# Attention: a unit's sums copied by two engines, half the columns each; root steps and turns moved in the projections

## The chip, the cores and the metric

The kernel runs on one core of a Trainium2 chip. The metric is the device time of one execution in microseconds, the median of several runs. The engines are TensorE (PE in the profile; its weight loads are PEld), VectorE (DVE), ScalarE (ACT), GpSimd (POOL) and SyncE (SP), which issues nearly all DMAs. Each engine works through its own queue in order; semaphores tie the queues together. TensorE writes its results into eight banks of PSUM, 512 float32 columns for each of 128 partitions.

## The reference

A transformer block on 2048 tokens of 640 numbers: layer norm, attention with 32 heads of 20 numbers, residual, layer norm, gated feed-forward of width 1728, residual.

```python
qkv = (x @ wqkv).reshape(B, S, 3, H, Dh).transpose(2, 0, 3, 1, 4)      # x: layer norm of the input
scores = jnp.einsum("bhqd,bhkd->bhqk", q, k) * (Dh ** -0.5)
p = softmax(scores, axis=-1)
o = jnp.einsum("bhqk,bhkd->bhqd", p, v)
h = x + o.transpose(0, 2, 1, 3).reshape(B, S, D) @ wo
h2 = h + (silu(n @ w_gate) * (n @ w_up)) @ w_down                      # n: layer norm of h
```

## The kernel before

**Three stages.** The projections (to about 325 us) make queries, keys and values; the attention (to about 1460 us) runs over 32 units; the rest is the output projection and the feed-forward part. Float32 is split into a high and a low part (`split`, L96: ScalarE copies the high part, another engine subtracts to get the low one, the "second part"), and products are the sum of three.

**The attention.** A unit `u` is a group of four heads and a chunk of 512 queries; it runs over 16 key tiles `kt`. A step of this loop has, for each head, one score product (`scores`, L1379, to a bank out of four) and its exponential on ScalarE (L1390); the weighing of the tile before it (`weigh`, L1392: probabilities times values, with a column of ones that yields the denominators), which adds up over the 16 tiles in one bank of its own (`acc`); and three maximum products for later units (`max_one`, L235, three banks in turn), each reduced by VectorE (L245). The order within a step is written out by hand in `ORDER`, three strings and their mirror images: `s` and `S` are scores, `m` and `M` maximum products, `W` the weighing, always last:

```python
ORDER = ("sMsSmSmW", "SmMsMsSW", "mSmMsSsW")
```

When the weighing of a unit's last tile is issued, in the first step of the next unit, `row_sums` (L1402) copies the bank to the tile `o` and lets SP bounce the rows of denominators (L1407); a few steps later they are inverted, spread over the heads' rows, multiplied in by GpSimd (L1429) and stored. There is one such bank, so the next unit's first weighing waits until the copy is done. VectorE's queue at this place holds the reductions of the step that ends, then, where a unit's maxima are complete, `max_all` (L249), then the reductions of the next step.

**The projections.** The tokens are taken in four chunks of 512. Work is a list of 72 slots: `first`, `none`, then `block` slots (a 128-row block of queries or keys of a chunk) and `value` slots. `begins(n)` is the slot at which chunk `n` is due: 10, 28 and 46. A planner, the class `Halves` (`pe`), keeps a modelled clock for each engine (`pe.free`, `pe.now()`) while the program is written and orders the instructions by it: products of the two halves of the array side by side, and in between, as filler, products of the maxima for which keys have landed. `second_part` (L661) chooses the engine of a second part by the modelled ends on GpSimd (1.3 us) and VectorE (0.75 us).

A chunk's tokens are normalized by items in the list `lns` (from `norm`, L759): four of statistics, six of the reciprocal root (Newton steps on VectorE, two instructions each, four numbers a row), four that apply it (VectorE for the first two chunks, GpSimd for the last two). Then come five turns (`flip`, L787): TensorE transposes a 128-column block of the chunk, ScalarE copies it twice, the second part follows. At the end of each slot the main loop issues up to two items (four in slots 4 to 6) and one turn, once all items are gone and the plan says that they are done; in the slot after `begins(n)` it issues all that are left, since the chunk's first block follows.

Of the kernel before, what the change touches and what calls it, by code (L numbers as in the profile page):

```python
# [13 lines left out]
AF = mybir.ActivationFunctionType  # L14
# [11 lines left out]
CH = 512  # L26
NC = S // CH
# [23 lines left out]
def tile_block(ctx: ExitStack, tc: tile.TileContext, x, wqkv, wo, wg, wu, wd, out):  # L51
    nc = tc.nc
# [77 lines left out]
    def stats(pool, src, mv):  # L130
        st = pool.tile([P, 2, 6], F32, name="st")
        for i in range(2):
            nc.vector.bn_stats(st[:, i, :], src[:, i * HALF : (i + 1) * HALF])  # L133
        nc.vector.bn_aggr(mv, st)


    NU = NG * NC
# [15 lines left out]
    ends = {}  # L153
# [185 lines left out]
    with tc.tile_pool(name="pa", bufs=2) as pa:  # L339
# [33 lines left out]
        def raw_place():  # L373
            return place(raw_tile().rearrange("p a b -> p (a b)")[:, : 2 * CH], nc.vector)
# [151 lines left out]
        def next_pair():  # L526
# [2 lines left out]
            queues = (others, early) if first else (early, others)  # L529
            return next((queue for queue in queues if queue and queue[0][0]()), None)  # L530

        SECOND = (("pool", 1.3), ("vector", 0.75))

        class Halves:
# [125 lines left out]

            def second_part(self, after):  # L661
                ends = [max(self.free[e], after, self.now()) + us for e, us in SECOND]
                if ends[1] + 1.0 < ends[0] and self.free["vector"] < after + 0.5:
                    return nc.vector, self.use("vector", SECOND[1][1], after)
                return nc.gpsimd, self.use("pool", SECOND[0][1], after)

# [70 lines left out]
        pe = Halves()  # L737
# [21 lines left out]
        def norm(c):  # L759

            mv = pa.tile([P, TPC, 2], F32, name="mv")
            r, steps = rstd_steps(pa, mv[:, :, 1], TPC, "a")

            def apply(t):
                (nc.gpsimd if c > 1 else nc.vector).tensor_scalar(
                    xs[c * TPC + t], xs[c * TPC + t], mv[:, t, 0:1], r[:, t : t + 1],
                    op0=ALU.subtract, op1=ALU.mult,
                )

            return (  # L770
                [
                    (("vector", 1.1), lambda t=t: stats(pa, xs[c * TPC + t], mv[:, t, :]), c)
                    for t in range(TPC)
                ]
                + [(("vector", 0.35), lambda f=f, g=g: (f(), g()), c) for f, g in zip(steps[::2], steps[1::2] + [lambda: None])]
                + [
                    (("pool", 2.55) if c > 1 else ("vector", 0.75), lambda t=t: apply(t), c)
                    for t in range(TPC)
                ]
            )  # L780
# [148 lines left out]
        def begins(c):  # L929
            return FIRST + (c - 1) * PHASE  # L930
# [9 lines left out]
        lns, flips, normed, x_at = [], [], 0.0, {1: 0.0}  # L940
        finish_at = len(work)
        for at, (kind, c, *which) in enumerate(work):
            slot[0] = at
            if at < 9:
                for i in range(split_at[at], split_at[at + 1]):
                    split_w(i + 2)
                    if i % 2 == 1 and loaded < 8:
                        load_w(loaded)
                        pe.sp(kb=655)
                        loaded += 1  # L950
            if at == 6:
                assert 9 not in raws
                own_places.insert(0, raw_place())
            if at == 9:
                assert not raws
                free_places.extend(raw_place() for _ in range(3))
            for n in range(1, NC):
                if at == (2 if n == 1 else begins(n) - 15):
                    lns = norm(n)
                if at == n == 1:  # L960
                    fill_rest()
                if n > 1 and at == begins(n) - 16:
                    assert not flips
                    load_x(n)
                    x_at[n] = pe.sp(n=4, kb=1310) + 0.3
            if kind == "first":
                first_blocks()
            elif which:
                (query_key if kind == "block" else value)(c, *which)
            for n in range(1, NC):  # L970
                if at == (7 if n == 1 else begins(n) - 3):
                    pe.finish_before(n - 1)
                    new_z(n)
                    flips = [(n, k) for k in range(ND)]
            if at == begins(NC - 1) + 15:
                pe.finish_before(NC - 1)
                z = zs[NC - 2][1]
                for i in (0, 2):
                    free_places.append(z[:, i : i + 2])
                z = pa.tile([P, ND, CH], F32R, name="z_hi")  # L980
                es += [z[:, :2], z[:, 2:4]]
                es[:] = [e for e in es if e is not stored(third)]
            if at == begins(NC - 1) + 4:
                assert not flips
                z = pa.tile([P, TPC, D], F32R, name="xt", bufs=1).rearrange("p t d -> p (t d)")
                free_places.extend(place(z[:, i * 2 * CH : (i + 1) * 2 * CH]) for i in range(2))
            if at >= LAST_QUARTER:
                for places in (free_places, own_places):
                    for i, q in enumerate(quarters):
                        if any(p is q for p in places):  # L990
                            places[:] = [p for p in places if p is not q]
                            cs = slice(i * CH, (i + 1) * CH)
                            fill_ones(k_stk[0], cs)
                            ready = pe.use("pool", 1.9, place_at.get(id(q), 0.0)) + 0.2
                            coming.append((ready, cs))
                            returned.append(i)
                back()
            for u, when in enumerate((5, begins(1) + 14, begins(2) + 14)):
                if at == when - 4:
                    es[:] = [e for e in es if all(e is not stored(q) for q in lent[:u])]  # L1000
                if at == when:
                    assert landed[0, 0, u] == GD
                    load_queries(u)
                    queries_at[u] = pe.sp(n=4, kb=750) + 4.5
            if 0 in ends:
                finish_at = min(finish_at, at + 2)
                if at == finish_at:
                    max_finish(0)
            if at == len(work) - 4:
                relus[:] = [r for r in relus if r is not third_relu]  # L1010
            if at == len(work) - 3:
                pe.finish_seconds()
                load_values(0, 0, NT - TPC)
            last = any(at == begins(n) + 1 for n in range(1, NC))
            for _ in range(99 if last else 4 if 4 <= at < 7 else 2):
                if at >= 2 and lns and (pe.now() >= x_at[lns[0][2]] or last):
                    normed = pe.use(*lns[0][0], normed) + 0.2
                    lns.pop(0)[1]()
            for _ in range(99 if last else 1):
                if flips and not lns and (pe.now() >= normed or last):  # L1020
                    flip(*flips.pop(0))
            if at == len(work) - 6:
                nc.scalar.activation(
                    pa.tile([P, 1], F32, name="exp_table"), eps_t, AF.Exp
                )
# [373 lines left out]
                tile_position=(0, 32 * j),  # L1399
            )  # L1400

    def row_sums(acc, *queues):  # L1402
        o = pc.tile([P, CH], F32, name="o", bufs=1)
        nc.scalar.activation(o, acc, AF.Copy)
        r = pc.tile([P, 16], F32, name="r")
        for j in range(G):
            queues[j % len(queues)].dma_start(  # L1407
                r[32 * j : 32 * j + 32, :],
                o[32 * j + DH : 32 * j + DH + 1, :].rearrange("r (p f) -> r p f", p=32),
            )  # L1410
        return o, r
# [24 lines left out]
    todo, tail, accs, closing, ended, now = [], [], {}, {}, [], [0]  # L1436
# [16 lines left out]
    def weigh_next():  # L1453
        u, kt, probs = todo.pop(0)
        if kt == 0:
            accs[u] = banks[:, acc_place]
        weigh(u, kt, probs, accs[u])
        if kt == NT - 1:
            queues = [nc.sync] if u + 1 < NU else [nc.scalar, nc.sync]
            tail.append((u, *row_sums(accs.pop(u), *queues)))  # L1460

    extra = []
    preparing = prepare_weights()
# [1 line left out]
    for u in range(NU):  # L1465
        g, c = divmod(u, NC)
        if g == NG - 1 and c >= 2:
            _, first, ln, flips, _ = ahead
            extra = [*first, *ln, lambda: None, *flips]
        for kt in range(NT):  # L1470
# [45 lines left out]
            if g == NG - 1 and c >= 1:  # L1516
                at = 8 if sooner else NT - 4
# [19 lines left out]
    while todo:  # L1537
        weigh_next()
    u, o, r = tail.pop()
# [466 lines left out]
    for e, (pair, f) in enumerate(ELEMENTS):  # L2006
        steps = 6 if f == NF - 1 else 8
        number, begin = RATES.get(e, (14 if e else 0, 0))
        each = spread_over(number, steps, begin)
        at = [0]  # L2010
# [90 lines left out]
```

## Time and profile before

| | us |
|---|---|
| runs (3): median, lowest, highest | 2024.7, 2023.99, 2026.38 |
| the profiled execution: its time, its span | 2026.52, 2024.7 |
| busy over the span: PE, DVE, ACT, POOL | 2002.5, 1620.2, 1460.2, 779.8 |

The span runs from the first to the last instruction of the profiled execution. Groups are read as: line, engine, operation, tile written <- tiles read, shapes, count | busy us in all, mean ns of one | idle us of the engine before them, and what ended it. In a timeline the first two numbers are the start and the length in microseconds, and "x4" means that four such instructions were put together. TensorE's clock was granted in full throughout.

### The profile page before, as it was taken

The page shows a single profiled execution, that of the slowest core. Times are in us where ns is not written, and L with a number is a line of the kernel's source. Part 1 is how long each engine was busy: PE and PEld are TensorE (multiplying, and loading weights), DVE is VectorE, ACT ScalarE, POOL GpSimd, SP SyncE. Part 2 cuts the span into 40 slices and gives each one's busy share as a digit, 9 for nine tenths or more (in the row PEclk, how much of TensorE's full clock was granted, in tenths as well). Part 3 has the DMA queues.
Part 4 walks back from the last instruction along what each step waited for, and adds up shares of the span by engine and source line. Part 5 has one row for each costly group of instructions (what it writes and reads, how often), then busy time and mean ns, then how long its engine had stood idle before and what let it go on. Part 6 is the DMA issues. An engine that isn't in the chain of part 4 may idle for free.

```text
span 2024.7 us, 39120 instructions
## 1 busy us (share of the span) xinstructions
PE 2002.5 (99%) x13714; PEld 1237.8 (61%) x13714; DVE 1620.2 (80%) x3257; ACT 1460.2 (72%) x2944; POOL 779.8 (39%) x1075
## 2 busy tenths in 40 slices
PE   8999999999999999999999999999999999999998
PEld 7898896333333333333333333345598888888888
DVE  8869678888888888888888888886378666676667
ACT  4888888999999999999999999986633222212221
POOL 4454451243524334344520011011146444764555
PEclk9999999999999999999999999999999999999999
DMA  7866663433443534435333122221159654974542
GB/s 234 257 198 192 190 191 108 135 116 117 140 128 106 161 117 142 145 123 166 123 134 102 33 71 73 81 62 49 46 185 323 206 189 154 352 272 159 204 148 93
DMA packets 205205, 304.91 MB, mean 151 GB/s; under 512 B 47648, under 2 KB 82720, under 8 KB 203984
## 3 DMA queue, kind: packets, MB, share of 16 engines
q1 hardware_dynamic: 204768, 302.24, 45.7%
q8 instruction: 109, 1.79, 0.4%
q14 instruction: 88, 0.72, 0.1%
q10 hardware_dynamic: 240, 0.17, 0.0%
HBM read 205.78 MB, written 95.68 MB: 149 GB/s over the span
## 4 chain that ended last, share of the span: by engine, by line
PE 95%; DVE 2%; ACT 1%; issue 1%; POOL 1%; DMA 0%; SPq 0%; ACTq 0%; DVEq 0%; POOLq 0%
PE banks L1394 25%; PE banks L1384 17%; PE banks L1562 17%; PE banks L239 12%; PE banks L573 9%; PE banks L1656 8%; PE banks L1113 3%; PE banks L218 3%; PE banks L195 1%; PE banks L836 0%; PE banks L264 0%; DVE st L133 0%; DMA o_t<-o_d 0%; PE banks L1145 0%; PE banks L793 0%
## 5 line engine op out<-in xcount | busy, mean ns | idle before, releaser
L1390 ACT ACTIVATE probs<-banks 128x512 f32<-128x512 f32 x2048 | 1056.2, 612 | 58.1 <-PE banks L1384 25.9
L245 DVE TENSOR_REDUCE mx<-banks 128x1 f32<-128x512 f32 x1472 | 925.1, 684 | 116.3 <-PE banks L239 62.6
L1384 PE MATMUL banks<-q_stk,k_stk 62*128 62x512 f32 x2048 | 581.3, 429 | 1.1 <-ACT probs L1390 1.1
L1394 PE MATMUL banks<-probs,v_stk 128*32 128x512 f32 x4096 | 544.3, 604 | 0.0
L239 PE MATMUL banks<-k_stk,q_stk 60*128 60x512 f32 x1472 | 486.5, 438 | 0.2
L1384 PEld LDWEIGHTS banks<-q_stk,k_stk 62*128 62x128 f32 x2048 | 290.4, 185 | 284.4 <-ACT probs L1390 270.3
L239 PEld LDWEIGHTS banks<-k_stk,q_stk 60*128 60x128 f32 x1472 | 244.2, 184 | 162.5 <-DVE mx L245 127.1
L1780 DVE TENSOR_TENSOR tmp<-banks,tmp 128x512 f32<-128x512 f32 x208 | 141.1, 689 | 114.5 <-PE banks L1562 89.0
L1394 PEld LDWEIGHTS banks<-probs,v_stk 128*32 128x32 f32 x4096 | 80.9, 108 | 182.0 <-issue 170.1
L1656 PE MATMUL banks<-halves,yp 128*128 128x320 f32 x1032 | 178.7, 308 | 0.2 <-DVE h L1661 0.2
L1656 PEld LDWEIGHTS banks<-halves,yp 128*128 128x128 f32 x1032 | 165.1, 188 | 16.0 <-DVE h L1661 0.5
L1562 PE MATMUL banks<-t,units 128*128 128x512 f32 x624 | 162.7, 396 | 0.1
L98 POOL TENSOR_TENSOR yp<-y,yp 128x256 fp32r<-128x256 f32 x96 | 60.5, 630 | 190.4 <-ACT yp L97 176.2
L1562 PE MATMUL banks<-z,units 128*128 128x512 f32 x516 | 133.7, 394 | 0.0
L256 POOL CAST both<-neg 128x16 fp32r<-128x16 f32 x32 | 6.6, 208 | 312.0 <-PE banks L239 187.1
L1562 PEld LDWEIGHTS banks<-t,units 128*128 128x128 f32 x624 | 112.5, 188 | 18.9 <-DVE tmp L1780 0.4
L1661 DVE TENSOR_TENSOR h<-banks,h 128x320 f32<-128x320 f32 x248 | 109.9, 480 | 8.6 <-POOL h L1694 4.3
L225 DVE CUSTOM_DVE_ANT_0 q_stk<-banks,q_stk 128x512 f32<-128x512 f32 x140 | 92.5, 687 | 24.1 <-PE banks L218 14.5
L573 PE MATMUL banks<-z_hi,w_hi 64*128 64x512 f32 x380 | 105.6, 396 | 2.3 <-ACT z_hi L97 2.0
L573 PE MATMUL banks<-z_lo,w_hi 64*128 64x512 f32 x380 | 105.2, 393 | 0.0
L1562 PEld LDWEIGHTS banks<-z,units 128*128 128x128 f32 x516 | 93.2, 187 | 15.9
L573 PE MATMUL banks<-z_hi,w_lo 64*128 64x512 f32 x380 | 101.8, 391 | 0.0
(218 smaller groups left out, 2900.8 us busy)
## 6 DMA issues: line engine op xcount, KB each, us to landing
units<-w_d SPq DMA_DIRECT2D x186, 256.0 KB
w_d<-stage SPq DMA_DIRECT2D x106, 256.0 KB
halves<-j_d SPq DMA_DIRECT2D x70, 320.0 KB
k_stk<-qk_d SPq DMA_DIRECT2D x112, 160.0 KB
j_d<-stage SPq DMA_DIRECT2D x42, 320.0 KB
q_stk<-qk_d SPq DMA_DIRECT2D x64, 160.0 KB
k_stk<-qk_d SPq DMA_DIRECT2D x112, 80.0 KB
rb<-r_d SPq DMA_DIRECT2D x32, 256.0 KB
```

The source lines that it names most:

```text
L218: nc.tensor.matmul(ps, q[rows, pair, t * P : (t + 1) * P], k[rows, pair, :], start=True, stop=True)
L225: nc.vector.tensor_tensor_reduce(out=place, in0=ps, in1=place, scale=1.0, scalar=LEAST, op0=ALU.add, op1=ALU.max, accum_out=mx[:, b, pair, ...
L239: nc.tensor.matmul(ps, queries[u][rows, pair, t * P : (t + 1) * P], keys[u // NC][rows, pair, kc * CH : (kc + 1) * CH], start=True, stop=True,
L245: nc.vector.tensor_reduce(mxs[u][:, b, pair, t, kc : kc + 1], ps, axis=AX.X, op=ALU.max)
L573: product = nc.tensor.matmul(job["ps"][:, :out], lhs, rhs, start=(half == 0 and i == 0), stop=(half == 1 and i == job["n"] - 1),)
L1384: nc.tensor.matmul(ps, keys[u // NC][rows, p, kt * P : (kt + 1) * P], queries[u][rows, p, :], start=True, stop=True,)
L1390: nc.scalar.activation(probs[p][:, b, :], ps, AF.Exp, scale=scale)
L1394: nc.tensor.matmul(acc[32 * j : 32 * j + 32, :], values[u // NC][:, kt, j * VW : j * VW + 32], probs[j // 2][:, j % 2, :], start=(kt == 0) ...
L1562: nc.tensor.matmul(ps.rearrange("p (t n) -> p t n", t=TPC), w[k][:, i], z[k][:, :, j], start=(first and m == 0), stop=(last and m == len(n ...
L1656: nc.tensor.matmul(ps, a, b, start=(n == 0), stop=(n == len(pairs) - 1))
L1661: nc.vector.tensor_tensor(out=h, in0=ps, in1=h, op=ALU.add)
L1780: add = lambda out, ps, x: nc.vector.tensor_tensor(out=out, in0=ps, in1=x, op=ALU.add)
```

## The change

The copy of a unit's sums is divided: ScalarE takes the first 256 columns, VectorE the other 256, except after the last unit, where ScalarE takes all as before. In the projections three rules of the planner change: VectorE's modelled end for a second part is never before GpSimd's own free time plus 0.75; a pair of root steps is issued only when GpSimd is free in the plan (or in the slot that issues all that is left); and in the slot `begins(n)` up to two turns are issued instead of one.

```diff
+        NEWTON = "vector", 0.35
         SECOND = (("pool", 1.3), ("vector", 0.75))
...
             def second_part(self, after):
                 ends = [max(self.free[e], after, self.now()) + us for e, us in SECOND]
+                ends[1] = max(ends[1], self.free["pool"] + SECOND[1][1])
                 if ends[1] + 1.0 < ends[0] and self.free["vector"] < after + 0.5:
                     return nc.vector, self.use("vector", SECOND[1][1], after)
                 return nc.gpsimd, self.use("pool", SECOND[0][1], after)
...
-                + [(("vector", 0.35), lambda f=f, g=g: (f(), g()), c) for f, g in zip(steps[::2], steps[1::2] + [lambda: None])]
+                + [(NEWTON, lambda f=f, g=g: (f(), g()), c) for f, g in zip(steps[::2], steps[1::2] + [lambda: None])]
...
             for _ in range(99 if last else 4 if 4 <= at < 7 else 2):
-                if at >= 2 and lns and (pe.now() >= x_at[lns[0][2]] or last):
+                alone = not lns or lns[0][0] != NEWTON or pe.free["pool"] <= pe.now()
+                if at >= 2 and lns and (pe.now() >= x_at[lns[0][2]] and alone or last):
                     normed = pe.use(*lns[0][0], normed) + 0.2
                     lns.pop(0)[1]()
-            for _ in range(99 if last else 1):
+            for _ in range(99 if last else 1 + any(at == begins(n) for n in range(1, NC))):
                 if flips and not lns and (pe.now() >= normed or last):
                     flip(*flips.pop(0))
...
-    def row_sums(acc, *queues):
+    def row_sums(u, acc, *queues):
         o = pc.tile([P, CH], F32, name="o", bufs=1)
-        nc.scalar.activation(o, acc, AF.Copy)
+        if u + 1 < NU:
+            nc.scalar.activation(o[:, : CH // 2], acc[:, : CH // 2], AF.Copy)
+            nc.vector.tensor_copy(o[:, CH // 2 :], acc[:, CH // 2 :])
+        else:
+            nc.scalar.activation(o, acc, AF.Copy)
...
-            tail.append((u, *row_sums(accs.pop(u), *queues)))
+            tail.append((u, *row_sums(u, accs.pop(u), *queues)))
```

## The prediction

> **What bounds the kernel now.** I read the times by stretch first, then the groups of instructions inside the attention, then the timeline around single unit boundaries, and last the idle times of TensorE in the projections.
>
> ```profile
> span 2024.7 us, 39120 instructions
> ```
>
> ```profile
> 45.00:122.00 77.00, 75.87 (x710) 70.29 (x708) 58.72 (x285) 60.33 (x173) 39.27 (x27) 1.00 0.75 235
> 122.00:204.00 82.00, 78.36 (x751) 72.52 (x749) 70.81 (x211) 70.41 (x135) 38.18 (x26) 1.00 0.63 195
> 204.00:288.00 84.00, 82.87 (x792) 75.65 (x790) 61.80 (x208) 72.19 (x148) 40.99 (x36) 1.00 0.61 187
> 327.00:1360.00 1033.00, 1033.00 (x7254) 407.07 (x7253) 914.85 (x1502) 1006.05 (x1986) 313.43 (x527) 1.00 0.35 111
> ```
>
> The columns are the stretch's length, then the busy time of PE, PEld, DVE, ACT and POOL, the granted clock and the DMA. The first three rows are the projections: PE is idle for 1.13 + 3.64 + 1.13 = 5.9 us there, and nothing else sets the pace, so an idle microsecond of PE taken away there is one off the end. The last row is the attention up to its last two units. PE is never idle, yet that is no proof that it is the limit, since a product that waits inside a step still counts as busy. The groups of that stretch tell more:
>
> ```profile
> L1390 ACT ACTIVATE probs<-banks 128x512 f32<-128x512 f32 x1924 | 992.0, 613 | 27.0 <-PE banks L1384 2.1 <-PE banks L239 0.3
> L245 DVE TENSOR_REDUCE mx<-banks 128x1 f32<-128x512 f32 x1441 | 905.9, 684 | 114.3 <-PE banks L239 62.6 <-PE banks L1384 47.8
> L1404 ACT ACTIVATE o<-banks 128x512 f32<-128x512 f32 x30 | 19.0, 633 | 0.0
> ```
>
> ScalarE is idle for 27 us in 1033, VectorE for 114. So PE and ScalarE run almost in lockstep and VectorE has little to spare. The step of the loop is read from the starts of the weighing (L1394), once per key tile:
>
> ```profile
> 468.66 0.64 PE L1394 MATMUL banks<-probs,v_stk 128*32 128x512 f32 x4
> 494.15 1.06 PE L1394 MATMUL banks<-probs,v_stk 128*32 128x512 f32 x8
> 498.42 1.06 PE L1394 MATMUL banks<-probs,v_stk 128*32 128x512 f32 x8
> 500.71 0.64 PE L1394 MATMUL banks<-probs,v_stk 128*32 128x512 f32 x4
> ```
>
> From 468.66 to 494.15 lie 12 steps: 25.49 / 12 = 2.124 us. The step right after the copy of a unit's sums, 498.42 to 500.71, takes 2.29. **About 0.17 us per unit boundary** is therefore all that the copy costs now. L1404 ran 30 times in this stretch, and the last of them falls into the mixed end, so 29 boundaries and 29 x 0.17 = 4.9 us are the most that the first edit can win.
>
> **First edit: the copy in halves.** ScalarE's copy shrinks from 512 to 256 columns; VectorE gets a new copy of 256 columns; the next unit's first weighing waits for both, and the bounce of the denominators by SP (L1407) too, which has no hurry, since the reciprocals come four key tiles later. No row shows this copy on VectorE, so I take the nearest ones (from the whole span):
>
> ```profile
> L206 ACT ACTIVATE q_stk<-banks 128x256 f32<-128x256 f32 x114 | 36.2, 386 | 7.1 <-PE banks L195 5.5 <-DVE mx L225 0.6 <-PE banks L573 0.5
> L1677 DVE COPY own<-banks 128x320 f32<-128x320 f32 x32 | 14.2, 480 | 0.4 <-PE banks L1656 0.4
> L208 DVE CUSTOM_DVE_ANT_0 q_stk<-banks,q_stk 128x256 f32<-128x256 f32 x114 | 42.1, 419 | 10.8 <-ACT q_stk L206 10.7
> ```
>
> ScalarE's half takes 0.386 us instead of 0.633: 0.25 off. VectorE's: between 320 columns (480 ns) and the reduction of 512 (684) lie 1.06 ns a column, so 256 take 0.41. Three reductions in a row last 1.89 us (below), 0.60 from start to start at 0.684 each, so a successor begins 0.08 before its predecessor's end: the copy holds VectorE for 0.33.
>
> Whether the two halves run **side by side or one after the other** decides the sign, and no row shows it. L206 and L208 are the nearest: each pair reads the two halves of one bank, ScalarE first, and VectorE's idle time before its half ends with ScalarE's instruction (10.7 of 10.8 us); but there VectorE also needs ScalarE's result. Nowhere does the trace show both engines inside one bank at once. I take one after the other, ScalarE first as in the code, and keep side by side as the other bound.
>
> The Trainium skill ("PSUM — Partial Sum Buffer", section "PSUM bank collisions raise a hardware error") says that ScalarE and VectorE reading one bank in the same partitions collide even in disjoint columns, and that such accesses must be ordered by semaphores. By that rule the side-by-side sum below cannot occur and the forecast's order holds; no run here shows it yet.
>
> Now one boundary, step by step:
>
> ```profile
> 531.96 0.63 ACT L1404 ACTIVATE o<-banks 128x512 f32<-128x512 f32 x1
> 532.20 1.89 DVE L245 TENSOR_REDUCE mx<-banks 128x1 f32<-128x512 f32 x3 [0.25 <-PE banks L239]
> 532.74 1.06 PE L1394 MATMUL banks<-probs,v_stk 128*32 128x512 f32 x8
> 533.85 0.48 PEld L239 LDWEIGHTS banks<-k_stk,q_stk 60*128 60x128 f32 x2
> 534.60 0.18 PEld L1384 LDWEIGHTS banks<-q_stk,k_stk 62*128 62x128 f32 x1 [0.16 <-ACT probs L1390]
> 535.03 0.64 PE L1394 MATMUL banks<-probs,v_stk 128*32 128x512 f32 x4
> ```
>
> Now VectorE stands idle for 0.25 us until 532.20 and then reduces three maximum products. The loss of this step sits at 534.60: the last score waits 0.16 for a bank, because ScalarE's exponentials run late by the copy. With halves in order, ScalarE is done at 531.96 + 0.39 = 532.35 and its exponentials come 0.25 earlier, so this wait goes. But VectorE's copy fills 532.35 to 532.68, and behind it in VectorE's queue stand the reductions: the first starts at 532.68, 0.48 late, and the third ends at 532.68 + 1.89 = 534.57 instead of 534.09. Maximum products have three banks in turn, so the third product of the next step (second load of the 533.85 row, which ends at 534.33 and so starts at 534.15, 0.06 after the third reduction) moves to 534.63. From that load to the next weighing lie 535.03 - 534.15 = 0.88, less the 0.16 that goes: 0.72. The weighing starts at 535.35, **0.32 later** than now. The same for the order "SmMsMsSW", whose third product stands two places later:
>
> ```profile
> 909.68 1.89 DVE L245 TENSOR_REDUCE mx<-banks 128x1 f32<-128x512 f32 x3 [0.26 <-PE banks L239]
> 911.62 0.18 PEld L239 LDWEIGHTS banks<-k_stk,q_stk 60*128 60x128 f32 x1
> 912.13 0.18 PEld L1384 LDWEIGHTS banks<-q_stk,k_stk 62*128 62x128 f32 x1 [0.31 <-ACT probs L1390]
> 912.56 0.64 PE L1394 MATMUL banks<-probs,v_stk 128*32 128x512 f32 x4
> ```
>
> The third reduction ends at 909.68 + 0.48 + 1.89 = 912.05, the load follows at 912.11, and 912.56 - 911.62 - 0.31 = 0.63 later the weighing: 912.74, **0.18 later**. In "sMsSmSmW" the third product is the last of the step, so it has the most room and I count 0. The three orders take turns at the boundaries: the mean is 0.17, 29 x 0.17 = 4.9 us. At 10 of the 29 boundaries VectorE's queue also holds the reduction of a unit's maxima:
>
> ```profile
> 497.68 0.22 DVE L252 TENSOR_REDUCE neg<-mx 128x16 f32<-128x64 f32 x1
> 498.06 3.21 DVE L245 TENSOR_REDUCE mx<-banks 128x1 f32<-128x512 f32 x5 [0.17 <-PE banks L1384]
> 500.00 0.18 PEld L239 LDWEIGHTS banks<-k_stk,q_stk 60*128 60x128 f32 x1 [0.29 <-DVE mx L245]
> ```
>
> This is the case that speaks loudest: one more small instruction (0.22) ahead of the reductions, and PE's load at 500.00 waits 0.29 for VectorE. There the delays add: 0.22 less the 0.08 of overlap, 10 x 0.14 = 1.4 us. **Sum of the first edit: +6.3 us.** Bounds: -4.9 (side by side: VectorE's 0.33 against an idle 0.25 delays its reductions by less than 0.1, and the loss of 0.17 goes) and 29 x 0.48 = +14 (VectorE's whole delay reaches PE at every boundary).
>
> **Second edit: the projections.** Adding pool's own end to VectorE's in `second_part` makes its condition unfulfillable: VectorE's end can never be more than 1.0 before GpSimd's, so every second part goes to GpSimd. The small root steps (NEWTON) wait until the plan has GpSimd free, and at the slot where a chunk begins two turns go out instead of one. The idle times of PE that bear on it:
>
> ```profile
> 54.12 0.68 PE L793 MATMUL banks<-ident,xt 64*128 64x64 f32 x5 [0.73 <-DVE mx L208]
> 132.32 0.41 PE L573 MATMUL banks<-w_hi,z_hi 64*128 64x320 f32 x1 [1.19 <-DVE mx L225]
> 141.87 0.50 PE L573 MATMUL banks<-z_hi,w_hi 64*128 64x512 f32 x1 [0.91 <-ACT z_hi L97]
> 163.98 0.50 PE L218 MATMUL banks<-raw,q_stk 60*128 60x512 f32 x1 [1.54 <-DVE mx L225]
> 225.48 0.50 PE L573 MATMUL banks<-z_hi,w_hi 64*128 64x512 f32 x1 [1.13 <-ACT z_hi L97]
> 129.85 1.81 DVE L98 TENSOR_TENSOR v_stk<-v_stk 128x512 fp32r<-128x512 f32 x1
> 159.40 1.24 DVE L107 TENSOR_SCALAR v_a<-mv 128x4 f32<-128x4 f32 x1
> L98 POOL TENSOR_TENSOR e<-e 128x512 fp32r<-128x512 f32 x15 | 19.5, 1297 | 53.3 <-ACT e L97 45.1 <-DMA xt<-qk_d 5.0 <-DMA raw<-qk_d 3.2
> ```
>
> A turn is eight transposes, three ScalarE instructions and one second part; it issues no DMA, and one slot earlier it stands ahead of that slot's products and of the stores that SP issues for them. Each edit has its stall. 132.32 and 54.12 follow a second part on VectorE (1.81 us at 129.85); on GpSimd such a part takes 1.30 and VectorE's sums are not behind it. 163.98 follows root steps of four numbers a row that last 1.24 each. 141.87 and 225.48 wait for the last turned block of a chunk, which one slot earlier would be ready. Together 0.73 + 1.19 + 0.91 + 1.54 + 1.13 = 5.5 us. Two things give back: all stores of projected blocks are now behind GpSimd, whose in-order queue holds four runs of 2.5 us of the normalization at a time, and the plan, which orders every product by its own clocks, comes out anew. I count **half, -2.7 us**; bounds -5.5 and +3 (as much new waiting as the half that I count).
>
> **The sum.** The profiled execution took 2026.5 us, its span 2024.7; the runs' median is 2024.7, 1.8 below that execution. 2026.5 + 6.3 - 2.7 = 2030.1 for an execution like it, **2028.3 us** for the median.
>
> **Rivals.** (1) Side by side: no order is put between the halves. For it: they share no byte. Against it: no such pair in the trace. 2024.7 - 4.9 - 2.7 = 2017. (2) VectorE's delay is taken up: its 114 us of idle time over some 486 steps are 0.24 a step, and ScalarE's earlier exponentials pay for the rest, so attention stays where it is: 2024.7 - 2.7 = 2022. Against it the load at 500.00. (3) The projections give all back while the attention loses: 2024.7 + 6.3 = 2031; for it the queue behind GpSimd. (4) The root steps find GpSimd busy slot after slot, until the slot after a chunk's begin flushes them:
>
> ```profile
> 105.36 2.50 POOL L765 TENSOR_SCALAR xt<-xt,mv,r_a 128x640 f32<-128x640 f32 x1
> 119.60 0.51 PE L793 MATMUL banks<-ident,xt 64*128 64x64 f32 x6
> ```
>
> The second chunk's normalization ends at 107.86, the first turn comes at 119.60: 11.7 us of room. Once the steps slip by more, four runs of 2.5 stand before the turns: +10, 2024.7 + 6.3 + 10 - 2.7 = 2038.3. GpSimd is busy for half of the time there, so several failures in a row are unlikely.
>
> **Chances.** Forecast 0.42 (own range 2025 to 2032), (1) 0.15, (2) 0.14, (3) 0.24, (4) 0.05. What a measurement can tell from no change is about 0.2%, 4 us: under 2020.7 is faster, over 2028.7 slower. Faster: nearly all of (1) and a little of (2), 0.17. Slower: half of the forecast, nearly all of (3), and (4): 0.48. Same: 0.35. The range 2017 to 2035 leaves out half of (1), all of (4) and the tails of (3).
>
> **What would show it.** In the timeline after: the start of VectorE's copy against the end of ScalarE's half (behind it: the forecast; beside it: rival 1); the step after each boundary, 2.29 now, 2.4 to 2.6 by the forecast and 2.12 by rival 1; a load of L239 that waits for VectorE in that step. In the projections: no root step over 1 us, no second part on VectorE, and the two waits for `z_hi` gone. A boundary step of 2.3 or less would prove the first half of the sum wrong, a stage before the attention that isn't shorter the second.

## The result, and the profile after

Over 20 runs of each the kernel before takes 2028.45 us (2023.99 to 2033.09) and the changed one 2031.05 (2027.46 to 2035.71). The ratio of the two is **1.0016, with a 95% interval of 1.001 to 1.0022**: slower by 3.2 us (2.0 to 4.5). The first three runs of the kernel before, on which the prediction stands, were on the low side. What can be compared is the difference: +3.6 forecast, +3.2 measured. The profiled execution of the changed kernel took 2031.65 us. The first row is its span on the page; the others are the same stretches as before (length, busy PE, PEld, DVE, ACT, POOL, clock, DMA).

```profile
span 2029.9 us, 39189 instructions
```

```profile
45.00:122.00 77.00, 75.51 (x727) 70.72 (x725) 57.08 (x284) 61.19 (x176) 42.83 (x30) 1.00 0.76 246
122.00:204.00 82.00, 82.00 (x798) 76.68 (x794) 63.25 (x208) 69.75 (x135) 44.71 (x32) 1.00 0.66 208
204.00:288.00 84.00, 82.18 (x756) 76.38 (x754) 63.99 (x216) 74.24 (x151) 38.53 (x34) 0.98 0.57 180
```

In the projections PE is now idle for 1.49 + 0 + 1.82 = 3.3 us instead of 5.9. The first weighing starts at 323.4 us of the span instead of 327.1. The attention loses more than that. From the first weighing of the second unit to that of the 31st of the 32, 29 units lie; they took 997.97 us before and take 1005.84: **+7.9 us**. The groups of the stretch 327 to 1360 us, kernel after (line engine operation out<-in count, busy and mean, idle before and its releasers):

```profile
L1393 ACT ACTIVATE probs<-banks 128x512 f32<-128x512 f32 x1912 | 990.0, 608 | 35.7 <-PE banks L1387 6.9 <-PE banks L239 2.8
L245 DVE TENSOR_REDUCE mx<-banks 128x1 f32<-128x512 f32 x1434 | 899.0, 684 | 100.9 <-PE banks L239 52.8 <-PE banks L1387 44.1
L1397 PEld LDWEIGHTS banks<-probs,v_stk 128*32 128x32 f32 x3824 | 75.1, 108 | 176.5 <-issue 161.2 <-DVE o L1409 15.0 <-DMA units<-w_d 0.4
L1409 DVE COPY o<-banks 128x256 f32<-128x256 f32 x29 | 12.3, 425 | 14.4 <-ACT o L1408 13.9 <-issue 0.5
L1408 ACT ACTIVATE o<-banks 128x256 f32<-128x256 f32 x29 | 12.1, 419 | 0.0
```

The same group of weight loads in the kernel before:

```profile
L1394 PEld LDWEIGHTS banks<-probs,v_stk 128*32 128x32 f32 x3848 | 75.5, 108 | 171.1 <-issue 159.4 <-ACT o L1404 10.5 <-DMA q_stk<-qk_d 0.4
```

ScalarE, the engine with the least room, got 7 us of copying less (19.0 busy before, 12.1 now), and stands idle for 9 us more (35.7 against 27.0). The half on VectorE waits 13.9 / 29 = 0.48 us each time for ScalarE's half: the halves go one after the other. And the weighing's loads wait 15.0 us for `o` instead of 10.5: PE gets the bank of the sums back later. The rows of one boundary that bear on it, from 528.27 (the last weighing of a unit) on, in the timeline of the kernel after:

```profile
528.27 1.07 PE L1397 MATMUL banks<-probs,v_stk 128*32 128x512 f32 x8
...
529.59 0.42 ACT L1408 ACTIVATE o<-banks 128x256 f32<-128x256 f32 x1
...
530.05 0.42 DVE L1409 COPY o<-banks 128x256 f32<-128x256 f32 x1 [0.45 <-ACT o L1408]
530.39 3.67 DVE L245 TENSOR_REDUCE mx<-banks 128x1 f32<-128x512 f32 x6
...
530.52 0.16 PEld L1397 LDWEIGHTS banks<-probs,v_stk 128*32 128x32 f32 x8 [0.49 <-DVE o L1409]
...
532.32 0.18 PEld L239 LDWEIGHTS banks<-k_stk,q_stk 60*128 60x128 f32 x1 [0.41 <-DVE mx L245]
...
532.89 2.22 ACT L1393 ACTIVATE probs<-banks 128x512 f32<-128x512 f32 x4 [0.20 <-PE banks L1387]
532.98 0.16 PEld L1397 LDWEIGHTS banks<-probs,v_stk 128*32 128x32 f32 x8 [0.37 <-issue]
```

VectorE idles 0.45 us, copies, and starts the reductions at 530.39, that is 0.80 after ScalarE's copy began; before it was 0.24 (531.96 to 532.20 in the prediction's rows). **Two** steps are long here. The one that ends in the copy, 528.27 to 530.52, takes 2.25, because the weighing waits for VectorE's half; before it took the usual 2.12. The one after it, 530.52 to 532.98, takes 2.46, because the load at 532.32 waits 0.41 for VectorE's reductions and ScalarE then stands idle; before 2.29. Worked out from the starts of the weighings of all 29 boundaries, the step after the copy went from 2.292 to 2.417 and the one before the next unit's weighing from 2.126 to 2.278. That is 0.125 + 0.152 = 0.277 per boundary, and 29 x 0.277 = 8.0: the whole loss of the attention. A step in the middle of a unit (key tiles 5 to 8) is unchanged, 2.123 before and 2.122 after.

The Trainium skill ("PSUM — Partial Sum Buffer", section "PSUM bank collisions raise a hardware error") demands that the accesses of two engines to one bank be ordered. All 31 copies of this trace agree with it: VectorE's half begins 0.03 us or more after ScalarE's has ended.

### The profile page after: what moved, and what is told of

Its sections match the earlier page's. It is cut to its first block, busy times and chain, and to the rows that moved or that the text cites. A ratio compares the mean times of both kernels' runs of the same rounds, so it can differ in the third digit from the quotient of the medians.

```text
span 2029.9 us, 39189 instructions
## 1 busy us (share of the span) xinstructions
PE 2005.9 (99%) x13714; PEld 1239.4 (61%) x13714; DVE 1616.6 (80%) x3281; ACT 1456.3 (72%) x2944; POOL 786.0 (39%) x1082
## 4 chain that ended last, share of the span: by engine, by line
PE 90%; DVE 4%; DMA 2%; ACT 2%; POOL 1%; issue 1%; SPq 0%; ACTq 0%; DVEq 0%; POOLq 0%
PE banks L1397 23%; PE banks L1569 16%; PE banks L1387 15%; PE banks L239 11%; PE banks L574 9%; PE banks L1663 8%; PE banks L1116 3%; PE banks L218 3%; DVE mx L245 2%; ACT probs L1393 1%; PE banks L195 1%; DMA xt<-in_A_x 1%; DVE o L1409 1%; DMA raw<-qk_d 0%; ACT o L1408 0%
## 5 line engine op out<-in xcount | busy, mean ns | idle before, releaser
L239 PE MATMUL banks<-k_stk,q_stk 60*128 60x512 f32 x1472 | 492.9, 439 | 1.7
```

Source lines behind the costliest of these rows:

```text
L239: nc.tensor.matmul(ps, queries[u][rows, pair, t * P : (t + 1) * P], keys[u // NC][rows, pair, kc * CH : (kc + 1) * CH], start=True, stop=True,
```

## The experiments

"Attention" below is the time of the same 29 units (before 997.97, after 1005.84), worked out from the starts of the weighings; "ratio" is against the kernel before, timed on the same chip.

### One half of the change at a time

```diff
  e1: row_sums as in the change (copy in halves), projections as before
  e2: the three projection hunks of the change, row_sums as before
```

> The kernel before with the copy in halves alone, the planner of the projections untouched. Theory A (order and queue: VectorE's copy starts when ScalarE's half ends, the reductions behind it in VectorE's queue come 0.57 us late, and TensorE's third maximum product of the next step waits for its bank): attention from the second unit's first weighing to the last unit's takes some 1005.8 us as in the changed kernel, against 998.0 before, the time is 7.9 us more, and the attention begins at 327 as before. Rival B (the two parts of the change work on each other, since another plan of the projections leaves other banks and other times to the attention): the attention's length differs from 1005.8 by more than 1 us.

> The changed kernel with the copy on ScalarE alone, as before: the edits of the projections alone. Theory A: the attention begins 3.7 us earlier (323.4 instead of 327.1), takes 998.0 as before, and the time is about 3.7 us less than before, 0.18 per cent. Rival B (the earlier begin is lost again in the attention): no less than before.

The halves alone: ratio 1.0036 (1.0023 to 1.0049), which is +7.3 us; attention 1005.54, both boundary steps as in the change (2.418 and 2.278). The projections alone: 0.9978 (0.9967 to 0.9988), which is -4.5 us (-6.7 to -2.4); attention 998.16. Together 7.3 - 4.5 = +2.8, against +3.2 for the change: the parts add up, and the loss sits in the copy alone.

### Is it the work on VectorE, or where it stands?

```diff
 # e3: VectorE copies all, no hand-over
+        if u + 1 < NU:
+            nc.vector.tensor_copy(o, acc)
 ...
 # e4: halves, VectorE issued first
+            nc.vector.tensor_copy(o[:, CH // 2 :], acc[:, CH // 2 :])
+            nc.scalar.activation(o[:, : CH // 2], acc[:, : CH // 2], AF.Copy)
```

> The kernel before with the whole copy on VectorE, 512 columns, except after the last unit. It waits for no other engine, so it should begin 0.45 us earlier than the half does, and hold VectorE for 0.60. Theory A (lateness of the reductions): they begin about 0.58 us after the place at which ScalarE's copy began, instead of 0.79 with halves and 0.22 before; ScalarE has 0.48 less to do; a loss of 0.06 a boundary, 2 us in all. Rival C (the bank of the sums is held longer, which delays the next weighing by 0.15): the bank is free at 0.65 to 0.70, as before, and nothing is lost. Rival D (VectorE's added work, whenever it comes): 0.60 added instead of 0.33, so nearly twice the loss of the halves, 14 us.

> The kernel before with the copy in halves, VectorE's half issued ahead of ScalarE's. Theory A: the order turns round; VectorE copies at once and its reductions come only 0.1 us late, but ScalarE stands idle for about 0.35 and its exponentials then run late by 0.6 to 0.7 instead of 0.48; the boundary step waits for ScalarE and no longer for VectorE, 0.15 to 0.2 a boundary more than before, 5 us in all. Rival D (VectorE's added work): as with halves, 8 us, and waits for VectorE. If the halves ran side by side whenever they could, neither engine would wait for the other and 4.9 us would be won.

With the whole copy on VectorE: ratio 0.9997 (0.9985 to 1.0008), attention 997.36, no loss at all, although VectorE's copy is 0.68 us long instead of 0.42. I had expected a loss of some 2 us from the lateness of the reductions, and it didn't come. Groups and timeline of this kernel:

```profile
L1394 PEld LDWEIGHTS banks<-probs,v_stk 128*32 128x32 f32 x3840 | 75.4, 108 | 173.6 <-issue 162.4 <-DVE o L1405 7.0 <-DVE neg L252 3.5
```

```profile
535.58 0.68 DVE L1405 COPY o<-banks 128x512 f32<-128x512 f32 x1
...
536.47 1.06 PE L1394 MATMUL banks<-probs,v_stk 128*32 128x512 f32 x8
...
538.78 1.07 PE L1394 MATMUL banks<-probs,v_stk 128*32 128x512 f32 x8
```

The copy starts without a wait, the bank is free as early as before (7.0 + 3.5 = 10.5 us of waiting for it, the 3.5 at boundaries where `neg` is named as the releaser), and the step after it takes 2.31 here and 2.270 in the mean (2.292 before). So a copy of 0.68 on VectorE, with ScalarE relieved of its 0.63, costs nothing: added work on VectorE, rival D, is not by itself the cause. With VectorE first, the ratio is 1.0008 (0.9999 to 1.0017) and the attention 1000.32:

```profile
L1394 PEld LDWEIGHTS banks<-probs,v_stk 128*32 128x32 f32 x3832 | 75.2, 108 | 170.9 <-issue 159.5 <-ACT o L1406 10.7 <-DMA units<-w_d 0.4
L1406 ACT ACTIVATE o<-banks 128x256 f32<-128x256 f32 x30 | 11.5, 384 | 5.8 <-DVE o L1405 5.8
```

```profile
535.36 0.18 PEld L1384 LDWEIGHTS banks<-q_stk,k_stk 62*128 62x128 f32 x1 [0.28 <-ACT probs L1390]
```

Here too the bank comes back in time (10.7), since VectorE, with its idle time, begins its half early and ScalarE waits only 5.8 / 30 = 0.19 us. What stays is a step of 2.37 after the copy, in all three orders nearly alike (2.35 to 2.39). Now ScalarE is the late one: at 535.36 the last score waits 0.28 for its exponentials. The halves in the other order cost the attention 2.4 us instead of 7.6; the expectation of +5 was too high. The loss depends on **which engine waits for the other**, and here the one with idle time should come first.

### The lateness of the reductions, without and with the held bank

```diff
 # e5: halves as in the change, and the boundary step takes the order whose
 # third product of the maxima is the last; e6: this alone; e7: this with e3
             order = ORDER[now[0] % len(ORDER)] if now[0] and (singles[0] or singles[1]) else "sSsSW"
+            if kt == 2 and u and order != "sSsSW":
+                order = ORDER[0] if order.count("m") == 2 else ORDER[3]
 # e8: ScalarE copies all; VectorE copies half of o once more, to a tile that nothing reads
+            nc.scalar.activation(o, acc, AF.Copy)
+            nc.vector.tensor_copy(pc.tile([P, CH // 2], F32, name="scratch", bufs=1), o[:, CH // 2 :])
```

> As the run with halves alone, and in each unit's third step (key tile 2, the one whose third maximum product waits for a late reduction) the order sMsSmSmW or its mirror image, in which that product stands last. Theory A (late reductions hold TensorE at the third product): the boundary step takes what it takes at the units that have this order already, 2.27 us, at every unit, instead of 2.27, 2.49 and 2.50; the step before it keeps its 2.28. From the second unit's first weighing to the last unit's: 1005.5 - 29 x 0.15 = 1001. Rival C (only the bank of the sums): no change, 1005.5.

> The kernel before with the order of that step alone. Theory A: before, the boundary step waits for ScalarE, not for VectorE, and takes 2.28 to 2.32 in every order; it stays so, 998.0 within 1 us. Rival: the order by itself is worth 4 us, and then the run with halves and order shows nothing of VectorE.

> The kernel before, ScalarE copying all 512 columns, and then VectorE copying 256 columns of the copy to a tile that nothing reads: VectorE waits for ScalarE and is late, but holds no bank. Theory A (late reductions): they begin about 0.9 us after the start of ScalarE's copy, later than with halves (0.79); the boundary step takes 2.5 to 2.6 in the two orders that feel it, the step before it stays at 2.12, and the stretch grows by 5 us or more. Rival C (the bank): the next weighing is not held, so 998 as before.

These three ran once each (2029.39, 2029.85 and 2039.66 us, beside a median of 2026.43 for the kernel before); the attention is read from their traces. In e5 the attention falls from 1005.5 to 1001.2. Its timeline, with the load that waits for the bank and the next weighing, and the group:

```profile
533.66 0.16 PEld L1394 LDWEIGHTS banks<-probs,v_stk 128*32 128x32 f32 x8 [0.50 <-DVE o L1406]
...
535.88 0.16 PEld L1394 LDWEIGHTS banks<-probs,v_stk 128*32 128x32 f32 x8 [0.24 <-issue]
```

```profile
L1394 PEld LDWEIGHTS banks<-probs,v_stk 128*32 128x32 f32 x3832 | 75.3, 108 | 175.1 <-issue 159.7 <-DVE o L1406 15.0 <-DMA units<-w_d 0.4
```

The step after the copy is 2.22 here and 2.262 in the mean of the boundaries, but 15.0 us of waiting for the bank and a step of 2.281 before it remain: the later place of the third product takes away the first loss and leaves the second. Without the halves the same order does nothing (e6: attention 997.93, boundary step 2.297), so it isn't a gain by itself. e8 is the reverse case, VectorE late and the bank free in time:

```profile
L1394 PEld LDWEIGHTS banks<-probs,v_stk 128*32 128x32 f32 x3800 | 74.6, 108 | 171.5 <-issue 160.3 <-ACT o L1405 10.5 <-DMA q_stk<-qk_d 0.4
```

```profile
395.93 0.63 ACT L1405 ACTIVATE o<-banks 128x512 f32<-128x512 f32 x1
396.59 0.29 DVE L1406 COPY scratch<-o 128x256 f32<-128x256 f32 x1 [0.74 <-ACT o L1405]
...
396.80 3.67 DVE L245 TENSOR_REDUCE mx<-banks 128x1 f32<-128x512 f32 x6
...
398.73 0.18 PEld L239 LDWEIGHTS banks<-k_stk,q_stk 60*128 60x128 f32 x1 [0.41 <-DVE mx L245]
```

The wait for the bank is 10.5 us again and the step before the copy 2.125, while the reductions start 0.87 after ScalarE's copy and the step after it takes 2.70 in the mean (2.50 to 2.89 by order, one boundary of 3.86 among them), more than the 2.5 to 2.6 expected. The attention takes 1011.44, +13.5. That size is not the price of lateness in the change: in e8 ScalarE still copies all 512 columns, so its exponentials are as late as before the change, and VectorE's reductions are late on top of that. But lateness and held bank are two separate prices: e8 shows lateness without the held bank, and e5 the held bank with most of the lateness gone.

### Both remedies, and the best version

> The whole copy on VectorE, with the order of that step. Theory A: at the units that have this order already the boundary step takes 2.155, against 2.31 and 2.36 at the others; all come to 2.155, the stretch to 997.4 - 29 x 0.115 = 994, 4 us under before, and the time with it. Rival: what is left at the others does not come from the third product, 997.

> The edits of the projections, the whole copy on VectorE, and the order sMsSmSmW or its mirror image in the third step of a unit. Theory A: the gains add: 4.5 us of the projections (2.4 to 6.7 by the measured interval) and 4.6 of the attention (993.4 against 998.0), 9 us less than before, a ratio of 0.9955; faster than the kernel before, the changed one and each of the two alone. Rival B: they don't add, 0.998.

VectorE copying all, with the third product late (e7): ratio 0.999 (0.998 to 0.9999), attention 993.37, and a step after the copy of 2.146: nearly a plain one. The 4.9 us that the prediction gave as the most that this edit could win are thus nearly all to be had (997.97 - 993.37 = 4.6), though not by halves. The timed gain, 2 us (0.2 to 4.1), is smaller than the attention's, and why isn't shown; the profiled execution lost 1.5 us in its first unit, told of at the end, but whether the other runs did isn't known. With the projection edits in addition (e12) the ratio is **0.9948 (0.9933 to 0.9963)**, 2017.22 us beside 2028.55, the best of all kernels here. Its weighings at one boundary of e7, and its span on the page of e12:

```profile
533.56 1.07 PE L1394 MATMUL banks<-probs,v_stk 128*32 128x512 f32 x8
535.67 1.07 PE L1394 MATMUL banks<-probs,v_stk 128*32 128x512 f32 x8
537.80 1.07 PE L1394 MATMUL banks<-probs,v_stk 128*32 128x512 f32 x8
```

```profile
span 2013.6 us, 39072 instructions
```

### The three rules of the projections, one at a time

```diff
  e9:  only  ends[1] = max(ends[1], self.free["pool"] + SECOND[1][1])
  e10: only  NEWTON and its condition
  e11: only  1 + any(at == begins(n) for n in range(1, NC))  turns
```

> The kernel before with the rule for second parts alone. Theory A (each edit of the projections takes away its own stall): no second part on VectorE after the first slots, and the idle times of TensorE near 54 us (0.73) and 132 us (1.19) are gone, those near 142, 164 and 225 stay; some 2 us less. Rival B (a new plan is a new lottery): the stalls come at other places and the time is anywhere within 3 us.

> The kernel before with the rule for the root steps alone. Theory A: no root step of the third and fourth chunk over 1 us, the idle time near 164 us (0.6 to 1.5 in the looks so far) is gone, the others stay; 0.5 to 1.5 us less. Rival B: as above.

> The kernel before with two turns in the slot at which a chunk begins, alone. Theory A: the waits of the chunk's first block for the last turned columns, near 142 us (0.91) and 225 us (1.13), are gone, the others stay; 2 us less. Rival B: they come back at the block's later products or at another place, since ScalarE, which copies the turned columns, is as busy as before.

| | ratio (interval) | in the stretch 45 to 290 us: second parts on VectorE; root steps over 0.3 us (seven and four before) |
|---|---|---|
| e9 | 0.9991 (0.9981 to 1.0001) | that of `w_lo` alone; five |
| e10 | 0.9988 (0.9977 to 0.9999) | ten with that of `w_lo`; none |
| e11 | 1.0026 (1.0016 to 1.0037) | six with that of `w_lo`; four |

By the ratios e9 is 1.8 us faster (from 3.9 faster to 0.2 slower, so not clear of no gain) and e10 2.4 us (0.2 to 4.7). In e9 the two stalls behind a second part are gone, those near 142, 164 and 225 us stay (1.28 at 145.1, 1.02 at 167.9, 1.03 at 228.1), and some below 0.5 us are new. In e10 the stall near 164 us is gone, as expected; against the expectation those near 132 and 225 us are gone too, and the one near 142 us has grown to 1.85. VectorE still takes second parts there, as the groups of the stretch 45 to 290 us show:

```profile
L98 DVE TENSOR_TENSOR v_stk<-v_stk 128x512 fp32r<-128x512 f32 x4 | 5.5, 1363 | 3.1 <-ACT v_stk L97 3.1
L107 DVE TENSOR_SCALAR r_a<-v_a 128x4 int32<-128x4 int32 x2 | 0.3, 170 | 0.1
```

e11 is the surprise: **slower**, by 5.3 us, although PE idles least of all kernels here:

```profile
45.00:122.00 77.00, 75.80 (x737) 71.14 (x738) 56.28 (x273) 60.19 (x172) 40.32 (x28) 1.00 0.77 243
122.00:204.00 82.00, 82.00 (x822) 76.04 (x820) 62.97 (x198) 68.89 (x138) 42.32 (x30) 1.00 0.65 199
204.00:288.00 84.00, 83.96 (x797) 77.73 (x795) 62.32 (x206) 70.68 (x141) 37.78 (x33) 1.00 0.63 194
290.00:309.00 19.00, 19.00 (x197) 18.48 (x194) 12.06 (x38) 12.30 (x24) 7.65 (x7) 1.00 0.82 236
309.00:329.70 20.70, 20.13 (x65) 11.60 (x63) 18.74 (x71) 17.61 (x38) 1.22 (x1) 0.62 0.29 90
```

Here PE is idle for 1.20 + 0 + 0.04 = 1.2 us up to 288, against 3.3 in the change. The last of the projections' own products starts at 309.3 (320.1 in the change, 323.8 before). But 54 of the 576 filler products, those of the maxima (L195 and L218), are left, where the other two kernels have none, and they run alone until 328.4, when the attention's first scores have begun. From 309 to 329.7 VectorE, which takes their maxima, is busy for 18.74 of 20.70 us and ScalarE for 17.61; PE gets through 65 products where 197 fitted into the 19 us before, at a granted clock of 0.62. The first weighing starts at 332.1, 5.0 us later than before. That the products left over are the loss is read from this one trace; no run tested it alone. The parts don't add up in this stage either: -0.9 - 1.2 + 2.6 = +0.5 per thousand singly, -2.2 together. Which of the other two rules restores the balance of filler and own products beside the two turns wasn't tried.

## Why the prediction held, and where it didn't

**One after the other, ScalarE first: shown.** The measured rows are 0.42 and 0.42 us, the hand-over 0.03 us (the median of the boundaries; 529.59 + 0.42 to 530.05 here), and the reductions begin 0.80 after ScalarE's start, where the sum had 0.39 + 0.33 = 0.72. Rival 1, side by side, is out, and with it its 2017.

**The loss after the copy: mechanism shown, single terms off.** The sum gave the three orders 0, 0.18 and 0.32, plus 0.14 at ten boundaries with `neg`, together 0.215 a boundary or 6.3 us. Measured at the boundaries without `neg` are -0.05 in "sMsSmSmW", +0.14 in "SmMsMsSW" and +0.18 in "mSmMsSsW", plus 0.12 with `neg`: 0.08 for the mean of the orders and 0.04 for `neg` give the 0.125 measured over all 29, 3.6 us. The term for "mSmMsSsW", 0.32, was nearly twice too large.

**What the sum left out: the held bank.** The prediction named that the next weighing waits for both copies, and priced nothing for it. Its own rows would have given a price: two copies in a row, 0.386 + 0.41 = 0.80, against 0.633 of one are 0.16 more; 0.152 a boundary was measured, 4.4 us. e5 keeps this loss and e8 is without it. Terms too large by 2.7 and one of 4.4 missing cancelled in part: 6.3 forecast, 7.9 in the trace, 7.3 timed in e1. The load that "waits for VectorE in that step", which was named as a sign, is there (0.41 at 532.32). The boundary step, forecast at 2.4 to 2.6, is 2.417 in the mean; the other lengthened step was not among the signs.

**Rival 2, the delay is taken up: out.** VectorE's idle time in the stretch fell from 114.3 to 100.9 us ahead of its reductions, so part of the copy went into it, but ScalarE's gain came back as idle time.

**The projections: right sign, too small.** Forecast -2.7, measured -4.5 (-6.7 to -2.4), near the bound of -5.5 and outside rival 3, by which they give all back. (The measured median of 2031.05 meets rival 3's 2031 only because the first three runs were low.) The half that was counted is what the idle time shows. In the eight profiled executions with the projections of before, PE idles between 45 and 288 us for 4.5 to 5.9 us, 5.3 in the mean; in the three with all three edits (the change, e2, e12) for 2.0 to 3.3, 2.7 in the mean: 2.6 less. The first weighing comes 4.7 us earlier in the mean of the same executions (322.7 instead of 327.4); where the other 2 us come from isn't shown.

The stalls at 54, 132, 142 and 164 us are gone. The 1.54 at 163.98 was a poor measure of the last one: of the other seven executions one has 1.52 there, four have 0.43 to 0.58, and two have none over 0.25. New is a wait for a sum on VectorE, 1.39 in this execution, 0.87 in e2 and none in e12:

```profile
76.59 0.49 PE L195 MATMUL banks<-raw 60*128 60x512 f32 x1 [1.39 <-DVE mx L208]
```

From 45 us on, no second part but that of `w_lo` runs on VectorE, but one root step over 1 us stays. It runs beside an instruction of GpSimd (L433, 80.22 to 81.52) at a place where the plan has GpSimd free; the root step just before it took 0.17:

```profile
80.36 1.19 DVE L107 TENSOR_SCALAR r_a<-v_a 128x4 int32<-128x4 int32 x1
```

**A step that failed** is that both waits for `z_hi` would go. The one of the third chunk is gone; that of the fourth stays and has grown, 1.15 + 0.65 instead of 1.13:

```profile
214.15 0.63 ACT L97 ACTIVATE z_hi<-xt 128x512 fp32r<-128x512 f32 x1
...
214.83 0.50 PE L574 MATMUL banks<-z_hi,w_hi 64*128 64x512 f32 x1 [1.15 <-ACT z_hi L97]
...
216.04 0.49 PE L574 MATMUL banks<-z_hi,w_hi 64*128 64x512 f32 x1 [0.65 <-ACT z_hi L97]
```

The turns' transposes ran at 211.1 and 211.6 us, but ScalarE, busy for 5.38 of the 6 us from 211 to 217, makes `z_hi` only at 214.15 and after. To issue a turn earlier in the program didn't make its copies early enough on ScalarE, which was the engine behind. Rival 4 didn't occur: the last root steps of the third and fourth chunk run at 98.8 and 180.7 us, and the turns of the third begin one by one, at 117.2, 122.5 and 127.5. (The rows by which rival 4 measures its room, at 105.36 and 119.60, belong to the third chunk, not the second.)

**The sum** came out within 0.4 us of the measured difference, from an attention loss too small by 1.0 to 1.6 and a gain too small by 1.8. That closeness is luck. The sign, the place and the order of the halves are not; of the attention's loss the sum had one of two parts.

## What to carry to other kernels

Dividing the emptying of a bank between two engines put the halves in a row here, in either order (e1, e4): the bank is held for the sum of both, and the second engine's queue stands still while it waits for the first. Price both, the hold for whoever writes the bank next, and the delay for what queues behind; give the whole copy to the engine with idle time, and move the product that depends on its queue to the end of the step. Idle time of TensorE is no measure of a stage with filler: count what filler is left when the own work ends.

## What the runs showed of the hardware

**Half clock after small waits.** After the two waits above, TensorE ran at half the clock for 3.4 us, in the windows of the kernel after:

```profile
211.00:217.00 6.00, 4.18 (x45) 3.34 (x44) 0.39 (x2) 5.38 (x12) 5.46 (x5) 0.98 0.78 249
216.80:220.20 3.40, 3.40 (x23) 3.40 (x20) 1.31 (x4) 1.12 (x3) 3.07 (x3) 0.50 0.54 184
```

PE was busy for 4.18 of the 6 us ahead of it, and the longest pause was 1.15. The Trainium skill ("TensorE: Matmul & The Clock Gate", section "What's actually happening") puts the clock down after an idle window of about 3.4 us; the 3.4 us of half clock agree with that length, but no pause of that length stands here. Nor do such pauses always bring it: e2 has the same two, 1.14 and 0.65, and the half clock behind them; e12 has them as well and keeps the full clock; and e10 has a pause of 1.85 with the full clock. The change shows another 3.4 us of half clock at 1452.4, where no pause in the 12 us before is longer than 0.45. e11 shows it at length, 0.62 of the clock over 20.7 us in which no more than 0.6 us of PE are idle. In that window 65 products count as 20.13 us of busy time, where 197 filled the 19 us before, more of a difference than the clock makes: the profile counts waiting inside a product as busy, so these rows don't tell what PE did, and the cause stays open.

**The stage before the attention varies from execution to execution.** In eight profiled executions with the projections of before, the first weighing stands at 325.6 to 329.3 us, by the same program for that stage. In e3 to e7 the first step of the attention is 3.5 to 3.7 us long instead of 2.1, and in each of the five the clock is at half for 3.4 us from there on; for e7 the stretch 329.3 to 337 has a granted clock of 0.78, which is 3.4 of 7.7 us at half. The three with all three edits (the change, e2, e12) have 321.0 to 323.6 and a first step of 2.1. A single execution can therefore not price an edit of 2 us in this stage, and the text goes by the timed ratios there.
